# Window attention into a soft mixture of experts: VectorE's small steps in one-tensor form, sink sums scaled once at the end, and new keys for the planner

## The chip, the cores and the metric

The kernel runs on one core of one Trainium2 chip. The metric is the device time of one execution in microseconds; the median of three runs is given with the lowest and the highest. The engines are TensorE (PE in the rows; PEld is its weight load), VectorE (DVE), ScalarE (ACT), GpSimd (POOL), and SyncE (SP), which only issues the transfers.

## The reference, cut to what matters

Everything is float32. Attention has 4 batches, 8 heads, 768 positions and 64 columns a head; a query sees the last 128 positions and the first 4, the sinks. Its output, 3072 tokens of 512 columns, goes through a soft mixture of 8 experts with 4 slots each.

```python
keep = is_sink | in_window                  # n_sink = 4, window = 128
scores = np.where(keep, q @ k.T / 8, -1e9)
a = np.exp(scores - scores.max(-1));  a /= a.sum(-1) + 1e-9
x = (a @ v) as 3072 tokens x 512

logits = x @ phi                            # 3072 x 32 slots
d = softmax(logits, over the tokens)        # 1e-9 added to the sum
slot_input = d.T @ x                        # 32 x 512
slot_out = relu(slot_input[e] @ w1[e]) @ w2[e]      # 512 -> 1024 -> 512, 8 experts
c = softmax(logits, over the slots)         # 1e-9 added to the sum
out = c @ slot_out                          # 3072 x 512
```

## The kernel before, in words

**Jobs.** The 768 positions of a batch are three jobs of 256 tokens, so there are 12 jobs (`window_path`, line 768). A job loads q, k and v, transposes q and k by TensorE (`prep`), and makes four score tiles (`softmax`, line 843), one for each group of four heads (`quad`) and half of the rows (`odd`), each with 68 or 132 window columns next to the sinks'. For a score tile VectorE masks and takes the maximum (`maxima`), ScalarE does four exponentials with their sums (`exps`), VectorE adds EPS to the four sums and takes reciprocals (`inverse`, lines 901 to 903, two tensors of four columns), GpSimd multiplies 128x528 weights by them and copies the sink weights to `sk`. In the first job of a batch VectorE has one or three more steps a tile. Two score tiles of one quad are transposed (`weights_transposed`), copied to `xws`, cut to the window by GpSimd's selections (`select`), and multiplied with v (`values`).

**Tokens.** Each job ends in `tokens` (line 337): logits of 256 tokens, a running minimum of negated maxima `m` (lines 371 to 375), exponentials, a transpose of `lt`, and products with the tokens. `sums` (line 419) keeps `acc[:, 0:256]` as a running weighted sum, scaled by `al` when the maximum moves. The sinks' values are not added to the tokens; their weights are summed in `acc[:, 256:384]` (`far`), 32 columns for each batch, and put in at the end. Before the change all columns of `far` that are in use are scaled by `al` in every job (line 424), so 32 to 128 columns. `totals` keeps the running sum of exponentials `z`. `slot_softmax` (line 519) does the softmax over slots of a finished batch, with an EPS step on six columns (`rs`, line 534). `finish` (line 449) joins the two halves of the partitions, and after it the two expert layers and the output follow (`tail`, line 588), for which 32 weight tiles of 1 MB are loaded, most of them during attention into free slots, the last 14 when attention has given its slots back.

**What sets the order.** Every step of attention is put into a `Plan` with a key, an engine and an estimated time (`add`). `Plan.order` (line 196) is a list scheduler: it goes through the steps by estimated times, takes on each engine the step that can start first, and among those that can start within a small margin the one with the lowest key. The keys are a table (`CFG`, line 706), 4 for each job plus an offset for each kind of step. The result is one fixed order for each engine; on the chip an engine takes its instructions in that order and waits on semaphores. Instructions that are put out this way all have line 156. Two PSUM tiles hold scores (`s`), four hold everything else (`w`), so a step that opens a tile also waits until an older one has been copied out.

Of the kernel before, what the change touches and what calls it, by code (L numbers as in the profile page):

```python
# [8 lines left out]
F32 = mybir.dt.float32  # L9
# [4 lines left out]
AF = mybir.ActivationFunctionType  # L14
ALU = mybir.AluOpType
# [4 lines left out]
P = 128  # L20
# [53 lines left out]
class Sinks:  # L74


    def __init__(self, nc, plan, pool, tmp, c, v, store):

        B = v.shape[0]
        self.nc, self.c, self.store = nc, c, store.rearrange("p (b s) -> p b s", b=B)  # L80
        self.sk = [pool.tile([P, P], F32, name=f"sk{i}") for i in range(2)]
        self.pst = pool.tile([P, P], F32, name="pst")
# [39 lines left out]
        plan.add(1.5, "D", 2.0, load, w=["v4"])  # L122
        plan.add(1.0, "G", 0.6, clear, w=["swide", "vphi", ("sk", 0), ("sk", 1)])
        plan.add(1.0, "G", 0.15, lambda e: nc.gpsimd.tensor_copy(tmp[:, 64:128], v4), r=["v4"], w=["v4b"])
# [183 lines left out]
class Moe:  # L308
# [6 lines left out]
    def __init__(self, nc, c, keep, work, pools, B):  # L315
        self.nc, self.c, self.keep, self.work, self.pools, self.B = nc, c, keep, work, pools, B

        self.lt = keep.tile([P, P], F32, name="lt")
        self.lb = keep.tile([P, 2, 2, 32], F32, name="lb")
        self.spare = keep.tile([P, P], F32, name="spare")  # L320
        self.sel = keep.tile([P, 2, 32], F32, name="sel")
        self.acc = keep.tile([P, 384], F32, name="acc")
        self.sinks = None

        t = keep.tile([P, 7], F32, name="sums")
        self.m, self.z, self.zb, self.al = t[:, 0:2], t[:, 2:3], t[:, 3:5], t[:, 5:7]
        self.n = 0
        self.cs, self.ct = {}, {}
        self.call = keep.tile([P, B, 6, 32], F32, name="call")
        self.si = keep.tile([P, 4, 32], F32, name="si")  # L330

        self.eps = keep.tile([P, 1], F32, name="eps")
        nc.gpsimd.memset(self.eps, 0.0)
        nc.gpsimd.memset(self.eps[64:96], EPS)
        nc.vector.memset(self.z, 0.0)

    def tokens(self, plan, keys, b, j, x, xn, blocks):
# [19 lines left out]
        def logits(e):  # L357
# [12 lines left out]
        key = next(k)  # L370
        plan.add(key, "V", 0.2, lambda e: nc.vector.tensor_reduce(
            new, L["tile"][:, 0:P], op=ALU.max, axis=AX.X, negate=True), r=[L["name"]], w=[("m", n % 2)])
        if n:
            plan.add(key, "V", 0.07, lambda e: nc.vector.tensor_tensor(new, new, old, op=ALU.min),
                     r=[("m", (n + 1) % 2)], w=[("m", n % 2)])
# [10 lines left out]
        else:  # L386
            next(k)
        plan.add(next(k), "P", 0.11, lambda e: nc.tensor.transpose(T["tile"][:, 0:P], lt, c.ident),
                 r=["lt0", "lt1"], w=[T["name"]], new=T)
# [56 lines left out]
        plan.add(next(k), "AV", (0.11, 0.13), logit, r=[T["name"]], w=[("lg", b, j, x) for x in blocks], last=T)  # L446
        plan.add(key, "V", 0.56 if sinks else 0.4, sums, r=[S["name"], aln], w=["acc"], last=S)

    def finish(self, plan, keys):
# [3 lines left out]
        nc, c, work = self.nc, self.c, self.work  # L453
        m, mo = self.m[:, (self.n - 1) % 2:(self.n - 1) % 2 + 1], self.m[:, self.n % 2:self.n % 2 + 1]
        W, Z, SI, D = plan.psum(), plan.psum(), plan.psum(), plan.psum()
        sinks = self.sinks
        f = work.tile([P, 1], F32, name="f")
        rz = self.rz = work.tile([P, 1], F32, name="rz")
# [39 lines left out]
        if sinks:  # L498
            key = next(k)
            plan.add(key, "P", 0.2, far, r=["sf", "acc"], w=["sd"], new=D)  # L500
            plan.add(key, "V", 0.2, lambda e: nc.vector.tensor_tensor(
# [17 lines left out]
    def slot_softmax(self, plan, key, b, names):  # L519
# [17 lines left out]
        plan.add(key, "V", 0.7, sums, w=[n])  # L537
        plan.add(key, "V", 0.3, lambda _: nc.vector.tensor_tensor(
# [143 lines left out]
class Weights:  # L682
# [8 lines left out]
    def load(self, t):  # L691
# [3 lines left out]
        else:  # L695
# [9 lines left out]
PT = 3  # L705
CFG = {'prep': [12.62, 12.36],
       'load': [62.54, -93.04],
       'v': [68.49, 63.17],
       'S': -12.9,
       'M': 126.11,  # L710
       'E': 297.18,
       'N': -191.46,
       'K0': 89.87,
       'T': [-201.07, -298.71],
       'K': -214.45,
       'sel': [89.25, -30.52, -145.68, -195.21],
       'val': [295.22, -19.77, 342.69, 369.69],
       'xn': [-57.94],
       'tok': [357.78, -262.56, 29.9, -50.0, 133.69, -75.28, 36.37, -51.64, -299.8, 208.29, -224.86],
       'sm': -143.04,  # L720
       'sinks': -181.93,
       'tr': [63.06, 25.65, 135.89, 140.0, 109.95, 86.26, 129.98, 2.55, 42.1, 2.21, 118.89, 92.88, 82.47, 53.92,
           125.08, 116.73, 96.95, 0.0, 138.66, 84.47, 128.65, 60.63, 120.33, 77.77, 78.14, 114.47, 21.23],
       'w': [105.83, 8.0],
       'fin': [287.49, -10.46, -125.39, -132.28, 35.33, -56.83, -2.84, 389.2, -90.55, 66.83, 472.81],
       'xn1': [40.22],
       'tok1': [-9.5, -16.36, 75.49, -213.58, -107.33, 247.29, -76.98, 179.88, 150.72, 361.93, -107.59]}


def window_path(ctx, tc, c, moe, q, k, v, phi, w1, w2, out):  # L730
# [31 lines left out]
    pts = [t[:, 528 * i:528 * i + 528].rearrange("p (a y) -> p a y", a=4) for i in range(PT)]  # L762
    small = t[:, 1840:1864].rearrange("p (g x y) -> p g x y", g=3, x=2)
    eps = t[:, 1864:1868]
    qt = fr.tile([P, 4, 256], F32, name="qt")
    nc.vector.memset(eps, EPS)

# [4 lines left out]
    def copy(e, o, i):  # L772
        (nc.scalar.copy if e == "A" else nc.vector.tensor_copy)(o, i)
# [69 lines left out]
    def softmax(keys, n, tl):  # L843
# [5 lines left out]
        s = plan.psum("s")  # L849
        nm, z = small[:, g % 3, 0], small[:, g % 3, 1]  # L850
        pt = pts[g % PT]
# [422 lines left out]
```

## Time and profile before

| | |
|---|---|
| median of 3 runs | 247.46 us (245.77 to 247.46) |
| the profiled execution | 248.19 us |
| its span, from the first to the last instruction | 246.5 us |
| mean granted TensorE clock in the span | 0.965 of full speed |

The four batches run from about 7.5 to 183 us, `finish` with the turning of the slot weights to 194, the expert layers to 232, and the output to 246.5. [...]

### The profile page before, as it was taken

What the parts mean: (1) busy time and instruction counts of PE and PEld (TensorE: products, weight loads), DVE (VectorE), ACT (ScalarE), POOL (GpSimd) and SP (SyncE); (2) the same over time, 40 slices, a digit from 0 to 9 for tenths busy, and PEclk for the clock granted to TensorE, in tenths of its full rate; (3) what the DMA queues carried; (4) which work ended last, traced back from release to release, by engine and by line L of the source; (5) the groups of instructions that cost most, each with busy time, mean ns of one, the idle gap of its engine ahead of it and who ended that gap; (6) DMA issues with size and microseconds to landing.
All of it is one profiled execution on the core that took longest, in us unless ns stands there. A gap on an engine that the chain in (4) does not pass through costs nothing.

```text
span 246.5 us, 9008 instructions
## 1 busy us (share of the span) xinstructions
PE 212.7 (86%) x3547; PEld 151.2 (61%) x3547; DVE 168.9 (69%) x455; ACT 150.4 (61%) x579; POOL 131.7 (53%) x247
## 2 busy tenths in 40 slices
PE   7866998998979799798979998898799999998830
PEld 7754676775657577575757766576578533655520
DVE  3387896789999778999956899999736411324240
ACT  2257699758988866898886579888634212123230
POOL 3048687954777785487776646867894160000000
PEclk9979799999999999999979999999999999999995
DMA  5497997788989778998996998983119999999896
GB/s 124 104 212 168 257 212 206 287 186 244 195 251 282 229 256 174 258 198 236 278 263 195 178 274 194 311 268 134 45 44 350 419 366 357 351 349 370 297 314 214
DMA packets 102965, 59.47 MB, mean 241 GB/s; under 512 B 76292, under 2 KB 98820, under 8 KB 102916
## 3 DMA queue, kind: packets, MB, share of 16 engines
q1 hardware_dynamic: 102916, 58.83, 82.9%
q8 instruction: 30, 0.49, 0.8%
q14 instruction: 19, 0.16, 0.2%
HBM read 52.53 MB, written 6.29 MB: 239 GB/s over the span
## 4 chain that ended last, share of the span: by engine, by line
PE 50%; DVE 21%; ACT 14%; DMA 5%; issue 4%; POOL 2%; ACTq 0%; DVEq 0%; POOLq 0%
PE w L156 35%; PE s L156 14%; ACT wt L156 11%; DVE wt L156 8%; DVE s L156 7%; DMA wt<-in_moe_w_dram 5%; DVE sums L156 2%; DVE first L156 2%; PE w L1226 2%; POOL wt L156 1%; DVE acc L156 1%; DVE rs L156 1%; ACT first L156 1%; ACT wt L659 0%; ACT lt L156 0%
## 5 line engine op out<-in xcount | busy, mean ns | idle before, releaser
L156 ACT ACTIVATE wt<-s,wt 128x132 f32<-128x132 f32 x192 | 68.9, 382 | 11.0 <-PE s L156 4.6
L156 POOL TENSOR_TENSOR wt<-wt 128x528 f32<-128x528 f32 x48 | 51.2, 1066 | 28.3 <-DVE wt L156 10.0
L156 POOL TENSOR_SCALAR_AFFINE_SELECT wt<-wt 128x512 f32<-128x512 f32 x88 | 54.0, 639 | 18.8 <-ACT wt L156 12.8
L156 PE MATMUL w<-wt 128*64 128x128 f32 (+2 forms) x548 | 51.3, 324 | 4.3 <-DVE wt L156 2.6
L156 PE MATMUL s<-wt,qt 64*64 64x196 f32 (+2 forms) x768 | 44.4, 332 | 6.7 <-ACT wt L156 5.5
L156 PEld LDWEIGHTS w<-wt 128*64 128x64 f32 (+1 forms) x548 | 37.0, 144 | 16.2 <-POOL wt L156 4.4
L156 ACT ACTIVATION_READ_ACCUMULATOR wt<-s,wt 128x1 f32 x192 | 41.6, 217 | 0.0
L156 ACT COPY wt<-w 128x512 f32<-128x512 f32 (+1 forms) x50 | 28.0, 573 | 12.8 <-PE w L156 9.2
L156 DVE TENSOR_REDUCE wt<-s 128x4 f32<-128x528 f32 x48 | 33.9, 707 | 1.7
L156 PEld LDWEIGHTS s<-wt,qt 64*64 64x64 f32 x768 | 26.0, 135 | 14.3 <-ACT wt L156 7.9
L156 PE MATMUL w<-ident,first 64*128 64x64 f32 x576 | 27.1, 229 | 0.6 <-ACT qt L156 0.2
L156 PEld LDWEIGHTS w<-ident,first 64*128 64x128 f32 x576 | 21.5, 139 | 9.6 <-issue 4.8
L156 PE MATMUL w<-ident,wt 64*128 64x64 f32 (+1 forms) x419 | 24.2, 237 | 3.1 <-POOL wt L156 2.0
L156 PEld LDWEIGHTS w<-ident,wt 64*128 64x128 f32 (+1 forms) x419 | 18.7, 144 | 10.8 <-issue 5.6
L156 DVE COPY first<-w 128x512 f32<-128x512 f32 x28 | 18.8, 678 | 7.2 <-PE w L156 7.2
L156 DVE COPY_PREDICATED s<-later,s 128x256 f32<-128x256 uint8 x48 | 20.2, 421 | 2.1 <-PE s L156 1.1
L156 DVE COPY wt<-w 128x512 f32<-128x512 f32 (+3 forms) x27 | 16.8, 623 | 6.8 <-ACT wt L156 4.3
L156 ACT ACTIVATE qt<-w 128x512 f32<-128x512 f32 (+1 forms) x23 | 13.2, 581 | 9.3 <-PE s L156 7.9
L156 PE MATMUL s<-wt 128*32 128x256 f32 x240 | 15.4, 381 | 0.9 <-DMA wt<-in_moe_w_dram 0.9
L156 ACT COPY first<-w 128x512 f32<-128x512 f32 x20 | 11.6, 605 | 7.0 <-PE w L156 7.0
L156 DVE TENSOR_TENSOR wt<-wt 128x4 f32<-128x4 f32 x48 | 13.6, 284 | 2.2 <-POOL wt L156 1.0
L156 PE MATMUL w<-wt,si 128*32 128x512 f32 x120 | 14.1, 594 | 0.2 <-DVE si L156 0.2
(130 smaller groups left out, 255.9 us busy)
## 6 DMA issues: line engine op xcount, KB each, us to landing
wt<-in_moe_w_dram SPq DMA_DIRECT2D x30, 1024.0 KB, 8.0
wt<-in_v_dram SPq DMA_DIRECT2D x24, 256.0 KB, 4.8
first<-in_q_dram SPq DMA_DIRECT2D x22, 256.0 KB, 3.9
first<-in_k_dram SPq DMA_DIRECT2D x22, 256.0 KB, 4.7
out_dram<-wt SPq DMA_DIRECT2D x4, 1024.0 KB, 8.6
first<-in_moe_w_dram SPq DMA_DIRECT2D x2, 1024.0 KB
out_dram<-wt SPq DMA_DIRECT2D x3, 512.0 KB
first<-in_k_dram SPq DMA_DIRECT2D x4, 128.0 KB, 2.4
```

What stands on the lines that cost most here:

```text
L156: return self.tc.keep_in_program_order(f(*args, **kw))
L1226: nc.tensor.matmul(t[:, 0:P], lhsT=c.ident, rhs=c.ident, start=True, stop=True)
```

## The change: what it does

Five things in the small steps, and a new table.

- EPS is added by `tensor_scalar`, with the constant in the instruction, where it was a `tensor_tensor` with a tensor of constants. It covers six columns, the four sums and two more, read as 3x2 and written as 2x3; the same form is used for the six columns in `slot_softmax`.
- The running minimum `min(new, old)` and the totals `z * al + zb` become `tensor_scalar` steps with the second operand as a per-partition scalar. `m` gets a column for each job, and keeps them all.
- `far` is no longer scaled in every job. Inside a batch the 32 columns of that batch are scaled in the step that adds to them. At the end the exponential `f` is taken for the last maximum of each of the four batches, and GpSimd multiplies `far`, 128x128, by it; the product with `sel` then follows. The column of `m` after the last batch's takes the place that `old` had.
- `sk` has 64 columns instead of 128, so 64 rows are transposed and copied to `pst`, and the lower half of `pst` is cleared once.
- Estimated times of seven steps are changed, and all keys in `CFG` but `w`.

```diff
-        self.sk = [pool.tile([P, P], F32, name=f"sk{i}") for i in range(2)]
+        self.sk = [pool.tile([P, 64], F32, name=f"sk{i}") for i in range(2)]
...
-            for t in self.sk:
-                nc.gpsimd.memset(t, 0.0)
+            nc.gpsimd.memset(self.pst[64:128], 0.0)
...
-        old, new = self.m[:, (n + 1) % 2:(n + 1) % 2 + 1], self.m[:, n % 2:n % 2 + 1]
+        old, new = self.m[:, n - 1:n], self.m[:, n:n + 1]
...
-            plan.add(key, "V", 0.07, lambda e: nc.vector.tensor_tensor(new, new, old, op=ALU.min),
+            plan.add(key, "V", 0.07, lambda e: nc.vector.tensor_scalar(new, new, old, None, op0=ALU.min),
...
-                if n:
-                    z1 = 32 * (b + (j > 0))
-                    nc.vector.tensor_scalar(far[:, 0:z1], far[:, 0:z1], al, None, op0=ALU.mult)
                 if j:
-                    nc.vector.tensor_tensor(d, d, S["tile"][:, 256:288], op=ALU.add)
+                    nc.vector.scalar_tensor_tensor(d, d, al, S["tile"][:, 256:288], op0=ALU.mult, op1=ALU.add)
...
-                nc.vector.scalar_tensor_tensor(z[64:128], z[64:128], al[64:128], zb[64:128],
-                                               op0=ALU.mult, op1=ALU.add)
+                nc.vector.tensor_scalar(z[64:128], z[64:128], al[64:128], zb[64:128], op0=ALU.mult, op1=ALU.add)
...
-        plan.add(next(k), "A", 0.3, lambda e: nc.scalar.activation(f, m, AF.Exp, bias=mo, scale=-1.0), r=mm, w=["f"])
+        plan.add(next(k), "A", 0.3, lambda e: nc.scalar.activation(
+            fb, self.m[:, each - 1:self.n:each], AF.Exp, bias=mo, scale=-1.0), r=mm, w=["f"])
...
-            nc.tensor.matmul(D["tile"][:, 0:64], lhsT=self.acc[:, 256:384], rhs=s2, start=True, stop=True)
+            nc.tensor.matmul(D["tile"][:, 0:64], lhsT=swap, rhs=sel.rearrange("p h s -> p (h s)"), start=True, stop=True)
...
+            plan.add(key, "G", 0.3, lambda e: nc.gpsimd.tensor_tensor(
+                self.si, self.acc[:, 256:384].rearrange("p (b s) -> p b s", b=self.B),
+                fb.unsqueeze(2).to_broadcast([P, self.B, 32]), op=ALU.mult), r=["f", "acc"], w=["far"])
...
-            nc.vector.tensor_scalar(rs, rs, EPS, None, op0=ALU.add)
+            nc.vector.tensor_scalar(rs.rearrange("p (x y) -> p x y", x=2), rs.rearrange("p (x y) -> p x y", x=3),
+                                    EPS, None, op0=ALU.add)
...
-            nc.vector.tensor_tensor(z, z, eps, op=ALU.add)
+            nc.vector.tensor_scalar(z6.rearrange("p (x y) -> p x y", x=2), z6.rearrange("p (x y) -> p x y", x=3),
+                                    EPS, None, op0=ALU.add)
...
-       'S': -12.9,
+       'S': -115.04,
```

The order in TensorE's queue, in the middle job of the third batch (some 121 to 130 us in the profile). `s<-wt,qt` is a score tile, `w<-ident,first_76` the transposes of q or k, `w<-ident,wt` the transposes of attention weights, `w<-wt` the values, `w<-ident,sk_165` and `w<-ident,lt` the transposes of sink weights and of `lt`, `w<-first_77,lb` the products with the tokens. Before:

```order
L156 MATMUL s<-wt,qt 64x196 x8
L156 MATMUL w<-ident,first_76 128x64 x16
L156 MATMUL s<-wt,qt 64x196 x8
L156 MATMUL w<-ident,wt 128x64 x16
L156 MATMUL w<-ident,sk_165 128x128
L156 MATMUL w<-ident,lt 128x128
L156 MATMUL w<-wt 64x2x2x64 x2
L156 MATMUL w<-wt 64x2x64 x4
```

The same place now, from the same score tile on:

```order
L155 MATMUL s<-wt,qt 64x196 x8
L155 MATMUL w<-wt 64x2x2x64 x2
L155 MATMUL w<-wt 64x2x64 x4
L155 MATMUL w<-wt 64x2x2x64 x2
L155 MATMUL w<-wt 64x2x64 x4
L155 MATMUL w<-ident,wt 128x64 x16
L155 MATMUL w<-ident,sk_165 64x128
L155 MATMUL w<-ident,lt 128x128
L155 MATMUL s<-wt,qt 64x196 x8
L155 MATMUL w<-ident,first_76 128x64 x16
L155 MATMUL w<-first_77,lb 32x256
```

The values of the first four heads (the four rows of `w<-wt`) have moved ahead, from behind the transpose of `lt` to right behind a score tile, ahead of the second transposes of attention weights; a score tile and the transposes of q and k that stood ahead of `lt` now stand behind it.

VectorE's queue at the end of a batch, where the softmax over slots of the batch before is done. `acc` holds the running sums, `wt<-wt` the EPS step and the reciprocals, `rs` the six sums of the slot softmax. Before:

```order
L156 TENSOR_SCALAR acc<-acc,sums 128x64
L156 TENSOR_TENSOR acc<-acc,w 128x32
L156 SCALAR_TENSOR_TENSOR acc<-acc,sums,w 128x256
L156 TENSOR_TENSOR wt<-wt 128x4
L156 RECIPROCAL wt<-wt 128x4
L156 TENSOR_REDUCE rs<-call 128x6
L156 TENSOR_SCALAR rs<-rs 128x6
L156 RECIPROCAL rs<-rs 128x6
```

Now:

```order
L155 SCALAR_TENSOR_TENSOR acc<-acc,sums,w 128x32
L155 SCALAR_TENSOR_TENSOR acc<-acc,sums,w 128x256
L155 TENSOR_SCALAR wt<-wt 128x6
L155 RECIPROCAL wt<-wt 128x4
L155 TENSOR_SCALAR qt<-w 128x2x4x64
L155 TENSOR_SCALAR wt<-wt 128x6
L155 RECIPROCAL wt<-wt 128x4
L155 TENSOR_REDUCE rs<-call 128x6
L155 TENSOR_SCALAR rs<-rs 128x6
L155 RECIPROCAL rs<-rs 128x6
```

The scaling of `acc` is gone and the addition behind it carries the scalar; the EPS steps are `TENSOR_SCALAR` on six columns; a scaling of q (`qt<-w`) and another EPS step now stand ahead of the slot softmax.

## Rows read from the trace of the kernel before

**Rows 1.** The page, part 1: busy time of each engine, its share of the span, and instructions.
```profile
PE 212.7 (86%) x3547; PEld 151.2 (61%) x3547; DVE 168.9 (69%) x455; ACT 150.4 (61%) x579; POOL 131.7 (53%) x247
```
**Rows 2.** Busy time by stretch, one stretch for each of the four batches, cut where a batch's first score tile starts (us from the span's start): length, busy us of PE, of its weight loads (PEld), of DVE, ACT and POOL with their instructions, the granted TensorE clock as a share of full speed, the DMA engines' busy share, GB/s.
```profile
7.50:50.22 42.72, 37.21 (x705) 27.75 (x706) 33.20 (x89) 29.25 (x122) 28.59 (x51) 0.92 0.83 207
50.22:93.11 42.89, 38.37 (x740) 28.38 (x741) 37.35 (x98) 34.55 (x138) 29.62 (x53) 1.00 0.86 235
93.11:137.34 44.23, 39.98 (x738) 29.42 (x740) 37.27 (x98) 34.61 (x138) 29.56 (x52) 0.96 0.89 230
137.34:182.87 45.53, 40.59 (x753) 29.76 (x751) 39.47 (x102) 35.08 (x144) 32.41 (x58) 1.00 0.65 180
```
**Rows 3.** The same view for the third batch, cut in two.
```profile
93.11:126.13 33.02, 28.86 (x549) 20.93 (x549) 30.73 (x79) 27.66 (x111) 21.05 (x37) 1.00 0.91 227
126.13:137.34 11.21, 11.11 (x189) 8.48 (x191) 6.54 (x19) 6.95 (x29) 8.51 (x16) 0.85 0.83 238
```
**Rows 4.** The chain of work that ended last, in order of time: start us, us, engine, tile written, line. The pieces on small VectorE steps, and the last long wait.
```profile
73.96 0.98 DVE rs L156
...
79.39 1.05 DVE sums L156
...
116.58 0.98 DVE rs L156
...
122.02 1.04 DVE sums L156
...
157.50 0.60 DVE wt L156
...
158.88 0.74 DVE acc L156
...
171.11 0.60 DVE wt L156
171.91 0.91 DVE acc L156 x3
...
216.09 11.39 DMA wt<-in_moe_w_dram
```
**Rows 5.** Groups of VectorE instructions: line, engine, operation, out<-in by tile names, out<-in as partitions x elements (of the first shape, where a group has several), count | busy us, mean ns of one | idle before.
```profile
L156 DVE TENSOR_TENSOR wt<-wt 128x4 f32<-128x4 f32 x48 | 13.6, 284 | 2.2 <-POOL wt L156 1.0 <-ACT wt L156 0.9
L156 DVE TENSOR_TENSOR sums<-sums 128x1 f32<-128x1 f32 x11 | 7.2, 659 | 0.4
L156 DVE SCALAR_TENSOR_TENSOR acc<-acc,sums,w 128x256 f32<-128x256 f32 x11 | 5.2, 474 | 0.2 <-issue 0.2
L156 DVE TENSOR_SCALAR acc<-acc,sums 128x32 f32<-128x32 f32 (+3 forms) x11 | 5.2, 469 | 0.0
L156 DVE TENSOR_SCALAR rs<-rs 128x6 f32<-128x6 f32 x4 | 3.1, 770 | 0.1
L156 DVE SCALAR_TENSOR_TENSOR sums<-sums 64x1 f32<-64x1 f32 x11 | 2.4, 219 | 1.2 <-ACT lt L156 0.9
L156 DVE TENSOR_TENSOR acc<-acc,w 128x32 f32<-128x32 f32 x8 | 1.5, 188 | 1.3 <-PE w L156 0.6
```
**Rows 6.** Timeline, VectorE (DVE) and GpSimd (POOL) side by side at three places: start us, us, engine, line, operation, tiles and shapes, count [idle before <- what ended it].
```profile
116.45 1.07 POOL L156 TENSOR_TENSOR wt<-wt 128x528 f32<-128x528 f32 x1 [0.48 <-DVE wt L156]
116.58 0.97 DVE L156 TENSOR_SCALAR rs<-rs 128x6 f32<-128x6 f32 x1
...
190.31 0.46 POOL L156 TENSOR_TENSOR qt<-call,qt 128x128 fp32r<-128x128 f32 x1
190.31 0.27 DVE L156 TENSOR_SCALAR rz<-sums,f,eps 128x1 f32<-128x1 f32 x1
190.50 0.31 DVE L156 TENSOR_SCALAR lt<-sel,f 128x64 f32<-128x64 f32 x1
...
195.61 0.17 DVE L156 TENSOR_SCALAR rs<-rs 128x6 f32<-128x6 f32 x1
```
**Rows 7.** Who TensorE (PE) waited for: us in total, times, longest us.
```profile
PE s L156 <- ACT wt L156: 5.5, 8, 1.0
PE w L156 <- DVE pst L156: 3.0, 3, 1.2
...
PE w L156 <- ACT lt L156: 2.3, 3, 1.5
```
**Rows 8.** Timeline of PE at two places in the third and fourth batch.
```profile
124.62 0.30 PE L156 MATMUL w<-ident,sk 128*128 128x128 f32 x1
126.13 0.33 PE L156 MATMUL w<-ident,lt 128*128 128x128 f32 x1 [1.21 <-DVE pst L156]
126.39 3.48 PE L156 MATMUL w<-wt 128*64 128x256 f32 x24
...
171.04 0.89 PE L156 MATMUL s<-wt,qt 64*64 64x196 f32 x16 [0.38 <-ACT wt L156]
172.33 1.96 PE L156 MATMUL w<-wt 128*64 128x256 f32 x24 [0.39 <-POOL wt L156]
```
**Rows 9.** Busy time by stretch around the end of attention, columns as in Rows 2.
```profile
168.00:184.00 16.00, 13.68 (x241) 10.06 (x241) 10.86 (x30) 10.20 (x41) 13.91 (x27) 1.00 0.12 31
188.00:216.00 28.00, 27.43 (x295) 14.53 (x298) 8.81 (x32) 5.91 (x20) 6.02 (x13) 1.00 1.04 372
```
**Rows 10.** Timeline of the DMA queue on SyncE: start us, us that the issues took, tiles, count.
```profile
182.87 2.80 SPq L156 DMA_DIRECT2D wt<-in_moe_w_dram  x4
```

More of the change, by code (lines that the diff above doesn't have):

```diff
@@ L122, in __init__ @@
         plan.add(1.5, "D", 2.0, load, w=["v4"])
-        plan.add(1.0, "G", 0.6, clear, w=["swide", "vphi", ("sk", 0), ("sk", 1)])
+        plan.add(1.0, "G", 0.6, clear, w=["swide", "vphi", "pst"])
         plan.add(1.0, "G", 0.15, lambda e: nc.gpsimd.tensor_copy(tmp[:, 64:128], v4), r=["v4"], w=["v4b"])
@@ L323, in __init__ @@
         self.sinks = None
-        t = keep.tile([P, 7], F32, name="sums")
-        self.m, self.z, self.zb, self.al = t[:, 0:2], t[:, 2:3], t[:, 3:5], t[:, 5:7]
+        t = keep.tile([P, 5 + 3 * B + 1], F32, name="sums")
+        self.z, self.zb, self.al, self.m = t[:, 0:1], t[:, 1:3], t[:, 3:5], t[:, 5:6 + 3 * B]
         self.n = 0
@@ L370, in tokens @@
         key = next(k)
-        plan.add(key, "V", 0.2, lambda e: nc.vector.tensor_reduce(
+        plan.add(key, "V", 0.24, lambda e: nc.vector.tensor_reduce(
             new, L["tile"][:, 0:P], op=ALU.max, axis=AX.X, negate=True), r=[L["name"]], w=[("m", n % 2)])
         if n:
-            plan.add(key, "V", 0.07, lambda e: nc.vector.tensor_tensor(new, new, old, op=ALU.min),
+            plan.add(key, "V", 0.07, lambda e: nc.vector.tensor_scalar(new, new, old, None, op0=ALU.min),
                      r=[("m", (n + 1) % 2)], w=[("m", n % 2)])
@@ L387, in tokens @@
             next(k)
-        plan.add(next(k), "P", 0.11, lambda e: nc.tensor.transpose(T["tile"][:, 0:P], lt, c.ident),
+        plan.add(next(k), "P", 0.16, lambda e: nc.tensor.transpose(T["tile"][:, 0:P], lt, c.ident),
                  r=["lt0", "lt1"], w=[T["name"]], new=T)
@@ L446, in tokens @@
         plan.add(next(k), "AV", (0.11, 0.13), logit, r=[T["name"]], w=[("lg", b, j, x) for x in blocks], last=T)
-        plan.add(key, "V", 0.56 if sinks else 0.4, sums, r=[S["name"], aln], w=["acc"], last=S)
+        plan.add(key, "V", 0.55 if sinks else 0.4, sums, r=[S["name"], aln], w=["acc"], last=S)
     def finish(self, plan, keys):
@@ L453, in finish @@
         nc, c, work = self.nc, self.c, self.work
-        m, mo = self.m[:, (self.n - 1) % 2:(self.n - 1) % 2 + 1], self.m[:, self.n % 2:self.n % 2 + 1]
+        m, mo = self.m[:, self.n - 1:self.n], self.m[:, self.n:self.n + 1]
+        each = self.n // self.B
         W, Z, SI, D = plan.psum(), plan.psum(), plan.psum(), plan.psum()
         sinks = self.sinks
-        f = work.tile([P, 1], F32, name="f")
+        fb = work.tile([P, self.B], F32, name="f")
+        f = fb[:, self.B - 1:self.B]
         rz = self.rz = work.tile([P, 1], F32, name="rz")
@@ L499, in finish @@
             key = next(k)
-            plan.add(key, "P", 0.2, far, r=["sf", "acc"], w=["sd"], new=D)
+            plan.add(key, "G", 0.3, lambda e: nc.gpsimd.tensor_tensor(
+                self.si, self.acc[:, 256:384].rearrange("p (b s) -> p b s", b=self.B),
+                fb.unsqueeze(2).to_broadcast([P, self.B, 32]), op=ALU.mult), r=["f", "acc"], w=["far"])
+            plan.add(key, "P", 0.2, far, r=["fsel", "far"], w=["sd"], new=D)
             plan.add(key, "V", 0.2, lambda e: nc.vector.tensor_tensor(
@@ L533, in sums @@
             nc.vector.reduce_sum(rs, e, axis=AX.X)
-            nc.vector.tensor_scalar(rs, rs, EPS, None, op0=ALU.add)
+            nc.vector.tensor_scalar(rs.rearrange("p (x y) -> p x y", x=2), rs.rearrange("p (x y) -> p x y", x=3),
+                                    EPS, None, op0=ALU.add)
             nc.vector.reciprocal(rs, rs)
-        plan.add(key, "V", 0.7, sums, w=[n])
+        plan.add(key, "V", 0.8, sums, w=[n])
         plan.add(key, "V", 0.3, lambda _: nc.vector.tensor_tensor(
@@ L705 @@
 PT = 3
-CFG = {'prep': [12.62, 12.36],
-       'load': [62.54, -93.04],
-       'v': [68.49, 63.17],
-       'S': -12.9,
[L710 to L723, printed above, removed]
+CFG = {'prep': [-3.73, -7.0],
+       'load': [0.46, -428.98],
+       'v': [7.74, 3.29],
+       'S': -115.04,
+       'M': 718.72,
+       'E': 1322.67,
+       'N': -75.85,
+       'K0': 31.16,
+       'T': [-339.17, -595.64],
+       'K': -285.3,
+       'sel': [-5.04, -200.0, -383.99, -1007.74],
+       'val': [-107.55, -214.89, 322.25, 132.7],
+       'xn': [-332.17],
+       'tok': [144.73, -116.92, -979.6, -778.5, -344.49, -105.13, -350.16, 137.16, -1629.96, -74.14, 490.19],
+       'sm': -932.4,
+       'sinks': -391.46,
+       'tr': [124.03, 52.03, 127.84, 57.95, 67.55, 99.05, 140.0, 101.82, 89.63, 4.44, 12.53, 8.73, 53.92, 110.96,
+           65.83, 4.35, 23.97, 119.7, 126.05, 16.24, 113.23, 49.39, 84.86, 67.65, 0.0, 24.53, 115.51],
        'w': [105.83, 8.0],
-       'fin': [287.49, -10.46, -125.39, -132.28, 35.33, -56.83, -2.84, 389.2, -90.55, 66.83, 472.81],
-       'xn1': [40.22],
-       'tok1': [-9.5, -16.36, 75.49, -213.58, -107.33, 247.29, -76.98, 179.88, 150.72, 361.93, -107.59]}
+       'fin': [-580.79, -346.71, 51.07, -445.39, -122.03, -358.66, -188.2, 444.45, 209.77, 673.01, 355.17],
+       'xn1': [-365.55],
+       'tok1': [-918.42, -491.6, 242.3, -332.63, -294.4, 729.29, -894.49, 361.24, 84.18, -10.6, -793.66]}
 def window_path(ctx, tc, c, moe, q, k, v, phi, w1, w2, out):
@@ L762, in window_path @@
     pts = [t[:, 528 * i:528 * i + 528].rearrange("p (a y) -> p a y", a=4) for i in range(PT)]
-    small = t[:, 1840:1864].rearrange("p (g x y) -> p g x y", g=3, x=2)
-    eps = t[:, 1864:1868]
+    small = t[:, 1840:1870].rearrange("p (g y) -> p g y", g=3)
     qt = fr.tile([P, 4, 256], F32, name="qt")
-    nc.vector.memset(eps, EPS)
+    nc.vector.memset(t[:, 1840:1870], 1.0)
     jobs = [(b, j) for b in range(B) for j in range(NJ)]
@@ L849, in softmax @@
         s = plan.psum("s")
-        nm, z = small[:, g % 3, 0], small[:, g % 3, 1]
+        nm, z, z6 = small[:, g % 3, 0:4], small[:, g % 3, 4:8], small[:, g % 3, 4:10]
         pt = pts[g % PT]
@@ L890, in maxima @@
                                     negate=True)
-        add(keys["M"], "V", 1.1 + (0.55 * (1 - odd) + 0.15) * (j == 0), maxima, r=[sn], w=[sn, nn])
+        add(keys["M"], "V", 1.08 + (1.1 - 0.8 * odd) * (j == 0), maxima, r=[sn], w=[sn, nn])
         def exps(e):
@@ L928, in sinks_transposed @@
         h = plan.psum()
-        add(key, "P", 0.15, lambda e: nc.tensor.transpose(h["tile"][:, 0:P], sinks.sk[n % 2], c.ident),
-            r=[("sk", n % 2)], w=[h["name"]], new=h)
-        add(key, "AV", (0.17, 0.2), lambda e: copy(e, sinks.pst, h["tile"][:, 0:P]), r=[h["name"]], w=["pst"], last=h)
+        add(key, "P", 0.15, lambda e: nc.tensor.transpose(h["tile"][0:64, 0:P], sinks.sk[n % 2], c.ident),
+            r=[("sk", n % 2)], w=[h["name"]], new=h, mode=HALVES)
+        add(key, "AV", (0.17, 0.2), lambda e: copy(e, sinks.pst[0:64], h["tile"][0:64, 0:P]),
+            r=[h["name"]], w=["pst"], last=h)
     def select(key, n, quad, i):
```

## The prediction

> **What bounds the kernel now.** I read the page's busy shares first, then busy time by stretch, then the chain of waits, then the groups of small VectorE steps, and last a timeline with VectorE and GpSimd side by side. No engine is full over the span: PE has 86%, VectorE 69%, GpSimd 53% [rows 1]. Cut by batch it looks different. Each of the four batches takes 43 to 46 us, and PE is busy in 37.2 to 40.6 of them; the idle rest is 5.5, 4.5, 4.3 and 4.9 us, 19.2 together [rows 2]. Inside the third batch the idle time lies in one place: from 93.1 to 126.1 us VectorE is busy for 30.7 of 33.0 us and PE for 28.9, and behind that PE is busy for 11.1 of 11.2 [rows 3]. So for three quarters of a batch VectorE sets the pace, and then PE does.
>
> The reader is to see next what VectorE does with that time. Adding a constant to four numbers takes 284 ns on average, taking the smaller of two columns 659, adding a constant to six columns 770, scaling a few columns of the far sums 469 [rows 5]. The same step on six columns took 0.17 us at 195.6 us, where GpSimd had nothing to do, and 0.97 at 116.6, where it began 0.13 us into a GpSimd multiplication of 1.07 and ended with it (116.45 + 1.07 = 117.52, against 117.55) [rows 6]. These are waits for GpSimd, not work. Several stand in the chain that ended last: 0.98 twice, 1.05 and 1.04, 0.60 twice, 0.74 and 0.91 [rows 4].
>
> Behind attention the end hangs on the weights. The chain's last long piece is a wait of 11.4 us for a weight transfer [rows 4]; the DMA engines are busy at 0.12 of their time from 168 to 184 us, since every slot is taken, and at full share from 188 to 216 [rows 9]. So attention's end releases the transfers (the last fourteen weight tiles begin at 182.9 us [rows 10]), and what attention saves is saved at the end, as long as the earlier transfers are done by then; the 16 nearly idle us before 184 are room for that.
>
> **The change, part by part.** The sum is made against the profiled execution, 248.19 us; the median shown is 0.73 lower.
>
> *Small steps in a plain form.* 48 additions of EPS now read six columns as 3x2 and write them as 2x3; I price one at 0.17, the undisturbed step on six columns [rows 6]. Bounds: 0.17, since undisturbed it is the same work, and 0.28, today's mean, if they still wait. 48 x (0.284 - 0.173) = 5.3 us of VectorE. The 11 minima become a one-column step whose second operand is a per-partition scalar. The nearest rows are 219 ns for the one-column step with one such scalar [rows 5] and 0.27 with two, at 190.31, which ran while a GpSimd multiplication ran beside it from 190.31 to 190.77 and did not wait [rows 6]; I take 0.22, bounds 0.17 (the quickest small step on SBUF columns in these rows) and 0.66. 11 x (0.659 - 0.22) = 4.8. The four steps on six columns in the slot softmax go from 0.77 to 0.17: 2.4. The running totals get two scalars instead of one: 0.27 for 0.22, 11 x 0.05 = 0.6 more.
>
> [...] The row at 190.31 shows such a step not waiting [rows 6]. [...]
>
> *Far sums.* 11 scalings of 0.469 go, 5.2 us; eight additions at 0.19 take a scalar along, between 0.19 and the 0.47 of the same form on 256 columns [rows 5], taken at 0.22, near the one with 32 columns: 0.2 more. In their place GpSimd multiplies 128x128 once at the end, like the 0.46 at 190.31 [rows 6], with a hop on either side some 0.5 us on the way to the first layer. I cost it at nothing: the weights' transfer is the late one there [rows 4, 9]; without that cover it costs 0.5.
>
> VectorE so sheds 5.3 + 4.8 + 2.4 - 0.6 + 5.2 - 0.2 = 16.9 of 168.9 us. What counts is what stood on the path. From the chain [rows 4]: two steps on rs, 2 x (0.98 - 0.17) = 1.6; two minima, 1.05 + 1.04 - 2 x 0.22 = 1.65; two EPS steps, 2 x (0.60 - 0.17) = 0.85; two scalings of acc, 0.74 and about 0.45 of the 0.91, 1.2; less some five totals at 0.05, 0.25. Together 5.0. PE is next: in the stretch of 33.0 us it has only 4.2 to give.
>
> *The order.* All keys are new. In the middle of a batch a column of score tiles stood close together, and the transpose of lt came straight behind two prep and score steps; now a value step stands between, and score tiles are spread. Three waits can be read off. The transpose of lt waits 1.21 us for the copy of pst, queued on VectorE; this kind is 3.0 in three times, of the 2.3 for lt about 0.7 lie in the steps that moved [rows 7, 8]: 3.7 can go. Score tiles wait 5.5 for ScalarE [rows 7]; I take a third, 1.8, since ScalarE's own work stays. Against it, the values of the first four heads now stand only four steps behind their weights' transposes, in eight jobs. Before, one job has that order, and there PE waited 0.39 us for GpSimd [rows 8]: 8 x 0.39 = 3.1 paid. Net -2.4; bounds +3 (nothing won, all paid) and -8 (all 3.7 and 5.5 won, little paid).
>
> *The rest.* Two clears of sk become one half clear on GpSimd at the start, and transposes and copies of sink rows cover 64 instead of 128 rows: same columns, nothing. [...]
>
> Sum: -5.0 - 2.4 = -7.4, so 240.8 in its own execution and 240.1 against the median of 247.46.
>
> **The rivals.** *PE fills up.* If VectorE's 16.9 us and the even order let two thirds of the 19.2 idle us go, 12.8 leave: 234.7. For it: PE was 99% busy wherever VectorE wasn't in the way [rows 3]. Against: PE is one queue in order, and its steps wait on chains through three engines.
>
> [...]
>
> *Absorbed.* The shed time lies beside PE's work and the order brings nothing: 2 us or less, 245.5 to 247.5. For it: 12 of the 16.9 us are not in the chain.
>
> *GpSimd late, slower.* Behind the transposes stand two copies and up to four selections, and now only a score step, transposes, logits and a score step cover them. If one multiplication of 1.07 us [rows 6] stands ahead of them in GpSimd's queue, each of the eight waits is 0.39 + 1.07 = 1.46, 11.7 in all; less 5.0 and 3.7, with nothing won for ScalarE the end comes 3.0 later: 250.5. It decides from a mean wait of 1.1 us (8.7 / 8). Against: GpSimd has 13 free us in each batch [rows 2].
>
> **How the numbers follow.** Within 1%, 245.0 to 249.9, is what a measurement of this kernel can hardly tell from no change. Chances: the forecast with its own range of 237 to 243, 0.50; PE fills up, 0.15; steps that still wait, 0.13; absorbed, 0.13; slower, 0.09. The first three are faster by over 1% but for a little of the third: 0.77 faster, 0.14 within, 0.09 slower. The range runs from 234.5, the filled PE, to 246.5, which takes in the steps that still wait and half of the absorbed.
>
> **What would show it.** Right: VectorE's busy time near 152 us; no EPS step, minimum or rs step above 0.3 us; batches of 40 to 41.5 us; the last weight tiles requested near 175.5 us instead of 182.9; the part behind that as long as it was. Wrong: a mean of the EPS steps near 0.28; PE's waits for GpSimd in front of values over 8 us; a batch still over 42; or a released tail that is longer by what attention saved, for then the transfers were the bound.

## The result, and the profile after

The changed kernel takes 234.68 us (median of 4 runs, 233.64 to 235.58) against 246.62 beside it: 0.9523 of the time, interval 0.9449 to 0.9597. Two later comparisons gave 0.9498 and 0.9423. That is some 12 us less, where 7.4 were forecast. Ratios here and below leave out disturbed executions (two of those further down took 329.63 and 384.3 us), so a ratio can differ a little from the quotient of two medians, which take in all executions. The profiled execution took 235.58 us, of which the span is 233.9.

First the page's busy shares of the changed kernel, which answer to [rows 1].

```profile
PE 207.8 (89%) x3545; PEld 148.9 (64%) x3545; DVE 150.2 (64%) x437; ACT 151.0 (65%) x586; POOL 133.0 (57%) x247
```

VectorE lost 18.7 us of busy time, PE 4.9. Then the four batches, columns as in [rows 2], and behind them the DMA queue's row for the first two of the last weight tiles, which answers to [rows 10].

```profile
7.00:46.67 39.67, 34.60 (x635) 25.89 (x635) 30.43 (x82) 26.68 (x112) 24.65 (x45) 0.91 0.80 192
46.67:87.34 40.67, 37.95 (x740) 28.23 (x741) 31.52 (x92) 34.70 (x139) 29.84 (x52) 1.00 0.91 248
87.34:124.78 37.44, 37.02 (x739) 27.84 (x742) 31.59 (x91) 34.62 (x140) 29.83 (x52) 1.00 1.02 260
124.78:170.68 45.90, 42.56 (x823) 31.71 (x823) 35.25 (x102) 37.97 (x155) 36.77 (x64) 1.00 0.79 216
```

```profile
170.68 1.55 SPq L155 DMA_DIRECT2D wt<-in_moe_w_dram  x2
```

What matters most is the third batch: PE is busy for 37.02 of 37.44 us, while VectorE has 5.9 us free. Beside [rows 2] the batches are 3.1, 2.2 and 6.8 us shorter and the fourth 0.4 longer (it now holds 823 matrix products for 753, since the new order puts its first score tile further ahead). PE's idle time in the four fell from 19.2 to 11.6 us (5.1, 2.7, 0.4 and 3.3). The weights are requested at 170.68 instead of 182.87, and from there to the end it is 63.2 us (before 63.6): what attention saved was saved at the end.

Next the small steps of VectorE, columns as in [rows 5].

```profile
L155 DVE TENSOR_SCALAR wt<-wt 128x6 f32<-128x6 f32 x48 | 9.3, 195 | 0.2
L155 DVE TENSOR_SCALAR sums<-sums 128x1 f32<-128x1 f32 x11 | 2.3, 206 | 0.3
L155 DVE TENSOR_SCALAR sums<-sums 64x1 f32<-64x1 f32 x11 | 3.0, 276 | 1.4 <-ACT lt L155 1.0
L155 DVE TENSOR_SCALAR rs<-rs 128x6 f32<-128x6 f32 x4 | 1.1, 271 | 0.1
L155 DVE SCALAR_TENSOR_TENSOR acc<-acc,sums,w 128x32 f32<-128x32 f32 x8 | 1.9, 238 | 0.4 <-PE w L155 0.4
```

The means are near those forecast. But three places in the timeline (VectorE and GpSimd side by side, as in [rows 6]) show that this isn't because the EPS form no longer waits.

```profile
71.79 0.16 DVE L155 TENSOR_SCALAR wt<-wt 128x6 f32<-128x6 f32 x1
72.30 1.07 POOL L155 TENSOR_TENSOR wt<-wt 128x528 f32<-128x528 f32 x1 [0.80 <-DVE wt L155]
73.03 0.37 DVE L155 TENSOR_SCALAR rs<-rs 128x6 f32<-128x6 f32 x1
...
110.07 1.07 POOL L155 TENSOR_TENSOR wt<-wt 128x528 f32<-128x528 f32 x1
110.42 0.74 DVE L155 TENSOR_SCALAR wt<-wt 128x6 f32<-128x6 f32 x1
```

At 73.03 the step on rs begins inside GpSimd's multiplication and ends 0.03 us behind it (73.40 against 73.37); at 110.42 an EPS step does the same (111.16 against 111.14). The one at 71.79 takes 0.16 because GpSimd stands idle: the multiplication that comes next is the one that waits for this step. Of the 48, only 5 take more than 0.2 us.

Last, who PE waited for, which answers to [rows 7], and behind it, from the timeline, GpSimd's selections and the values of the first four heads in one job: the place at which the forecast paid.

```profile
PE s L155 <- ACT wt L155: 2.8, 5, 1.0
PE w L155 <- ACT lt L155: 1.5, 1, 1.5
PE w L155 <- POOL wt L155: 1.5, 1, 1.5
PE w L155 <- DVE pst L155: 0.7, 1, 0.7
```

```profile
113.11 2.52 POOL L155 TENSOR_SCALAR_AFFINE_SELECT wt<-wt 128x512 f32<-128x512 f32 x4
115.68 1.96 PE L155 MATMUL w<-wt 128*64 128x256 f32 x24
```

The one wait of 1.5 us for GpSimd's wt is in front of a transpose at the very start (12.94), not at values. The selections end at 115.63 and the values start at 115.68, just in time, without a wait.

### The profile page after: what moved, and what is told of

The parts are those of the page before. It is cut to its first block, busy times and chain, and to the rows that moved or that the text cites. A ratio compares the mean times of both kernels' runs of the same rounds, so it can differ in the third digit from the quotient of the medians.

```text
span 233.9 us, 8934 instructions
## 1 busy us (share of the span) xinstructions
PE 207.8 (89%) x3545; PEld 148.9 (64%) x3545; DVE 150.2 (64%) x437; ACT 151.0 (65%) x586; POOL 133.0 (57%) x247
## 4 chain that ended last, share of the span: by engine, by line
PE 69%; DVE 9%; DMA 8%; ACT 5%; issue 3%; POOL 2%; SPq 0%; DVEq 0%; POOLq 0%; ACTq 0%
PE w L155 49%; PE s L155 18%; DMA wt<-in_moe_w_dram 5%; ACT wt L155 3%; DVE s L155 3%; DVE wt L155 3%; DMA wt<-in_v_dram 2%; PE w L1229 2%; POOL wt L155 1%; DVE sums L155 1%; DVE first L155 1%; ACT wt L661 1%; ACT qt L155 0%; ACT pst L155 0%; DVE phi L155 0%
## 5 line engine op out<-in xcount | busy, mean ns | idle before, releaser
L155 POOL TENSOR_TENSOR wt<-wt 128x528 f32<-128x528 f32 x48 | 51.2, 1066 | 27.1 <-DVE wt L155 10.5
L155 PE MATMUL w<-wt 128*64 128x128 f32 (+2 forms) x548 | 49.6, 316 | 2.8 <-DVE wt L646 1.2
L155 PE MATMUL s<-wt,qt 64*64 64x196 f32 (+2 forms) x768 | 45.9, 337 | 5.2 <-ACT wt L155 2.8
L155 PEld LDWEIGHTS w<-wt 128*64 128x64 f32 (+1 forms) x548 | 35.4, 140 | 15.8 <-POOL wt L155 2.5
L155 ACT ACTIVATION_READ_ACCUMULATOR wt<-s,wt 128x1 f32 x192 | 41.5, 216 | 0.0
L155 ACT COPY wt<-w 128x512 f32<-128x512 f32 (+1 forms) x48 | 27.4, 578 | 13.6 <-PE w L155 10.2
L155 PEld LDWEIGHTS s<-wt,qt 64*64 64x64 f32 x768 | 26.9, 137 | 12.8 <-ACT wt L155 3.9
L155 DVE COPY wt<-w 128x512 f32<-128x512 f32 (+3 forms) x29 | 18.2, 627 | 16.0 <-PE w L155 11.8
L155 ACT COPY first<-w 128x512 f32<-128x512 f32 x33 | 19.0, 598 | 10.4 <-PE w L155 10.1
L155 PE MATMUL w<-first,phi 128*32 128x128 f32 x384 | 13.0, 276 | 0.0
L155 ACT ACTIVATE qt<-w 128x512 f32<-128x512 f32 (+1 forms) x19 | 11.0, 585 | 2.5 <-PE s L155 1.6
L155 PEld LDWEIGHTS s<-wt 128*32 128x32 f32 x240 | 7.9, 110 | 7.1 <-DMA wt<-in_moe_w_dram 1.3
```

Of the source, the lines that this page charges most:

```text
L155: return self.tc.keep_in_program_order(f(*args, **kw))
```

## The experiments

The question was where the extra 4 to 5 us came from: from the small steps (the forecast gave them 5.0) or from the order (2.4). The code is shortened throughout.

**Steps and order apart.** Two kernels, each with one half of the change. In the first, the keys and time estimates of before are put back; in the second, the steps of before run under the new keys and estimates. The estimated times that differ between the two kernels are five, not seven. But for the clears at the start and the finish, whose far sums differ, the queues of PE and GpSimd stand in the traces as in the kernel whose order is used. So does ScalarE's with the order alone. With the steps alone three of its copies of transposed weights stand with VectorE instead (26 copies of 128x512 to `wt` for 23 before, 2.0 us): the planner may give such a copy to either engine.

```
steps_old_order: the changed kernel, with
-CFG = {'prep': [-3.73, -7.0], ...
+CFG = {'prep': [12.62, 12.36], ...          (and the five estimates of before)
order_old_steps: the kernel before, with
-CFG = {'prep': [12.62, 12.36], ...
+CFG = {'prep': [-3.73, -7.0], ...           (and the five new estimates and the mode of the sink transposes)
```

Of the steps alone was expected: 

> All new small steps (EPS in 3x2 to 2x3, minima with a scalar operand, far sums scaled once by GpSimd, half-height sink rows), but the keys and time estimates of the kernel before, so that the queues of PE, ScalarE, GpSimd and SP stand as they did before. If the two parts of the forecast simply add, the steps are worth 5.0 us: 241.6 against 246.6. If the steps carry nearly all (VectorE was the pace and PE fills up in any order): 235 to 237. If the order carries nearly all: 244 to 246.

Of the order alone: 

> All old small steps, but the keys and time estimates of the changed kernel, so that the queues of PE, ScalarE, GpSimd and SP stand as they do after. If the two parts add, the order is worth 2.4 us: 244.2. If the order carries nearly all: 236 to 239. If the order rests on the quick steps (values placed close behind their weights' transposes then wait for GpSimd, whose multiplications wait for the slow EPS steps): 245 to 250, with PE's waits for GpSimd above the 7.5 us of before.

Of the changed kernel beside them: 

> The changed kernel once more, beside its own variants: 233.6 to 235.6 under every theory.

Measured against 247.12 us: the steps alone 243.25, 0.9885 (0.9849 to 0.9921); the order alone 236.67, 0.9641 (0.9566 to 0.9715); both 233.62, 0.9498 (0.9435 to 0.9561). So by the ratios the steps are worth 2.8 us, the order 8.9 and both 12.4: they add nearly, with the sizes the other way round. The split is rough, since it hangs on the kernel before: by the medians alone the steps come to 3.9 and the order to 10.5. Without the kernel before, the order is worth 9.6 us with the new steps (243.25 to 233.62), and the steps 3.1 in the new order (236.67 to 233.62). That the order rests on the quick steps is out. VectorE's groups show what either half does, first the steps alone, then the order alone; `first<-w` are the copies of transposed q and k.

```profile
L155 DVE TENSOR_SCALAR wt<-wt 128x6 f32<-128x6 f32 x48 | 15.7, 328 | 3.6 <-ACT wt L155 2.4 <-POOL wt L155 1.0
L155 DVE TENSOR_SCALAR sums<-sums 128x1 f32<-128x1 f32 x11 | 2.4, 214 | 0.4
L155 DVE TENSOR_SCALAR rs<-rs 128x6 f32<-128x6 f32 x4 | 0.8, 195 | 0.1
L155 DVE COPY first<-w 128x512 f32<-128x512 f32 x28 | 18.8, 676 | 4.2 <-PE w L155 4.2
```

```profile
L156 DVE TENSOR_TENSOR wt<-wt 128x4 f32<-128x4 f32 x48 | 9.7, 201 | 0.2
L156 DVE TENSOR_TENSOR sums<-sums 128x1 f32<-128x1 f32 x11 | 2.5, 231 | 0.3
L156 DVE TENSOR_SCALAR acc<-acc,sums 128x32 f32<-128x32 f32 (+3 forms) x11 | 3.6, 325 | 0.0
L156 DVE TENSOR_SCALAR rs<-rs 128x6 f32<-128x6 f32 x4 | 1.1, 270 | 0.1
L156 DVE SCALAR_TENSOR_TENSOR sums<-sums 64x1 f32<-64x1 f32 x11 | 4.8, 437 | 1.5 <-ACT lt L156 1.1
L156 DVE COPY first<-w 128x512 f32<-128x512 f32 x15 | 10.1, 676 | 3.3 <-PE w L156 3.2
```

In the old order the new EPS form takes 328 ns, more than the old form's 284 [rows 5]. In the new order most old forms have little wait left: 284 to 201, 659 to 231, 770 to 270. The totals go the other way: 219 before, 437 in the new order, where they meet GpSimd's steps (the one at 116.13 takes 1.04 us and ends at 117.17, a multiplication at 117.16). Counted in the timelines, 18 of the 48 EPS steps took more than 0.2 us before, 26 with the steps alone, 7 with the order alone and 5 with both. The order, not the form, took most of the waits away. The order does one more thing: 13 of the 28 copies of transposed q and k that VectorE made before, 8.7 us, are now ScalarE's, while four more scalings of q, 2.7 us, have come to VectorE. The minimum is a step whose form did take the wait away. Its place in the old order, with the new form, is the twin of the 1.05 us at 79.39 in [rows 4]; timeline of the steps alone:

```profile
77.21 1.07 POOL L155 TENSOR_TENSOR wt<-wt 128x528 f32<-128x528 f32 x1 [0.41 <-DVE sums L155]
77.24 0.21 DVE L155 TENSOR_SCALAR sums<-sums 128x1 f32<-128x1 f32 x1
```

It begins 0.03 us into the multiplication and is done in 0.21 us.

**Does the EPS step's shape matter, and do its waits carry the order's gain?** In the built changed kernel the contiguous 3x2 and 2x3 stand merged: its trace records a run of six read and a run of six written, though the views print 128x6 for either shape. With the unmerged strides below it records three pairs read and two triples written. Three kernels in the order of before: without the step, with strides that can't be merged, and with five columns in one run.

```
-nc.vector.tensor_scalar(z6 as 2x3, z6 as 3x2, EPS, None, op0=ALU.add)
no_eps_old_order: (nothing)
+odd_old_order:  nc.vector.tensor_scalar(zo[2 rows of 4][:, :, 0:3], zi[3 rows of 3][:, :, 0:2], EPS, ...)
+five_old_order: nc.vector.tensor_scalar(z5, z5, EPS, None, op0=ALU.add)
```

Without it: 

> The new small steps in the order of before, without the 48 EPS additions (each sum holds a term exp(0) = 1, and 1 + 1e-9 is 1 in fp32). In the old order these steps took 15.7 us of VectorE (48 x 0.328). If the order's gain of about 8.9 us comes through VectorE (in the new order its small steps find GpSimd idle, so they don't wait), taking the waiting steps out of the old order must bring most of it: 235 to 238. If the gain is PE's own sequence (fewer waits for the copies of pst, for ScalarE, for the weights), the old order stays at 241 to 243.

Unmerged: 

> The new small steps in the order of before, the EPS addition with strides that can't be merged: three pairs at distance 3 read, two triples at distance 4 written. In the built changed kernel the contiguous 3x2 and 2x3 stand as one run of six. If the shape on the engine decides whether the step waits for GpSimd: mean 0.16 to 0.18 us instead of 0.328, and the time within 1 us of the kernel without the steps plus at most 48 x 0.17 of VectorE. If every such step waits, whatever its shape: 0.30 to 0.33, and 241 to 244.

Five: 

> The new small steps in the order of before, the EPS addition over five columns in one run (odd, and the same for source and destination) instead of six. If an odd count alone frees the step from waiting: mean 0.16 to 0.18 us and a time as with the unmerged strides. If odd but equal waits as even does: 0.30 to 0.33 us and 241 to 244.

Measured against 247.47 us: without 237.64, 0.9619 (0.9588 to 0.9650); unmerged 240.03, 0.9708 (0.9671 to 0.9745); five 243.33, 0.9841 (0.9812 to 0.9870). The groups, unmerged and then five:

```profile
L155 DVE TENSOR_SCALAR wt<-wt 128x6 f32<-128x6 f32 x48 | 7.3, 152 | 3.2 <-ACT wt L155 3.2
```

```profile
L155 DVE TENSOR_SCALAR wt<-wt 128x5 f32<-128x5 f32 x48 | 16.0, 333 | 3.6 <-ACT wt L155 2.4 <-POOL wt L155 1.0
```

The same step at the same place, in the timeline of the steps alone and then of the unmerged form:

```profile
106.21 0.64 POOL L155 TENSOR_SCALAR_AFFINE_SELECT wt<-wt 128x512 f32<-128x512 f32 x1
106.33 0.54 DVE L155 TENSOR_SCALAR wt<-wt 128x6 f32<-128x6 f32 x1
```

```profile
106.04 0.63 POOL L155 TENSOR_SCALAR_AFFINE_SELECT wt<-wt 128x512 f32<-128x512 f32 x1
106.13 0.15 DVE L155 TENSOR_SCALAR wt<-wt 128x6 f32<-128x6 f32 x1
```

As one run of six it ends with GpSimd's selection (106.87 against 106.85); unmerged it is done in 0.15 us in the middle of one. So at this place the shape that reaches the engine decides (0.54 us against 0.15; over the 48 steps a mean of 328 ns against 152), and the change's own shape never reached it. The run of five, which waits as the run of six does, gained 3.9 us; the unmerged form, which doesn't wait, some 7 (0.9708). So in the old order the waits of the EPS steps are worth 3.3 us (243.33 to 240.03), and the steps themselves, without a wait, another 2.4 (240.03 to 237.64). Without the step the old order comes to 0.9619, as good as the new order with all the old steps (0.9641). The windows of its two middle batches, beside those of the steps alone:

```profile
48.74:88.56 39.82, 37.65 (x738) 27.87 (x735) 32.32 (x84) 33.54 (x137) 29.68 (x51) 1.00 0.95 254
88.56:128.38 39.82, 37.65 (x739) 27.87 (x735) 32.33 (x84) 33.53 (x137) 29.67 (x51) 1.00 0.96 246
```

```profile
49.04:90.11 41.07, 38.10 (x737) 28.14 (x734) 35.49 (x96) 33.53 (x137) 29.77 (x52) 1.00 0.89 245
90.11:131.17 41.06, 38.11 (x738) 28.14 (x734) 35.48 (x96) 33.53 (x137) 29.68 (x52) 1.00 0.97 245
```

Each batch is 1.25 us shorter, with 3.2 us less of VectorE. It is still 2.2 us longer than PE is busy.

**The small steps in the new order.** Five kernels with the changed kernel's order, each with one thing undone or taken further.

```
eps_two:        +nc.vector.tensor_tensor(z, z, eps, op=ALU.add)
far_each:       +nc.vector.tensor_scalar(far[:, 0:z1], far[:, 0:z1], al, None, op0=ALU.mult)   (in each step; plain additions)
min_totals_two: +nc.vector.tensor_tensor(new, new, old, op=ALU.min)   (and the totals with one scalar)
odd:            the unmerged EPS step as above
no_eps:         without the EPS step
```

> The changed kernel with its order, only the 48 EPS additions as a step of two SBUF tensors again (four columns plus four columns). If VectorE's time is now cover (64% busy, PE the bound): within 1 us of the changed kernel, 234 to 236. If the EPS steps stand on the path to GpSimd's multiplication and so to PE's transposes of the weights: 48 x 0.1 to 0.12 us come back in part, 237 to 240, and PE's waits for GpSimd rise from 4.1 to 8 us or more. Their mean should go from 195 ns to 280 or more under both.

> The changed kernel with its order, but the far sums scaled in each step again (11 scalings) and added plainly; GpSimd's multiplication at the end uses one factor. If the far sums carry the difference of about 3 us between old and new small steps in the new order: 235.5 to 237. If VectorE's time is cover there: within 1 us of the changed kernel, 233 to 235, with scalings of 0.26 to 0.5 us, 3 to 5 us of VectorE in all.

> The changed kernel with its order, but the 11 minima as a step of two tensors and the 11 totals with one scalar and one tensor, as before. In the new order with all old steps these took 231 and 437 ns against 206 and 276 now: 11 x 0.19 = 2 us of VectorE. If they are what the new small steps are worth in the new order (3 us between old and new steps there): 235 to 236.5. If nothing of it is on the path: 233 to 235.

> The changed kernel with its order and the EPS additions in strides that can't be merged (pairs read, triples written). In the new order these steps took 195 ns, 40 more than the 152 that the unmerged form took: 2 us of VectorE, nearly all beside PE's work: 232.5 to 235. A time under 232 would say that the few long steps (up to 0.74 us) stand on the path.

> The changed kernel with its order, without the 48 EPS additions (each sum holds exp(0) = 1, so 1e-9 is lost in fp32). Beside the old order without them (0.962 of before) it shows what the order is worth where these steps can't wait. If the order works only by keeping small steps off GpSimd's: no better than the old order without them by over 1 us, 236 to 238. If PE's own sequence is worth something as well: 232 to 234. VectorE loses 9.3 us of busy time; if that time is cover, as the run with the two-tensor form suggests, the time is that of the changed kernel within 1 us.

The changed kernel beside the last three: 

> The changed kernel a third time, beside these variants: 233 to 235.5 under every theory, 0.945 to 0.955 of before.

Measured: two-tensor EPS 234.16, 0.9525 (0.9445 to 0.9606); far sums in each step 234.42, 0.9473 (0.9438 to 0.9508); old minima and totals 233.02, 0.9428 (0.9371 to 0.9485); unmerged EPS 234.53, 0.9483 (0.9425 to 0.9542); no EPS 232.86, 0.9443 (0.9394 to 0.9492); the changed kernel a third time 232.48, 0.9423 (0.9387 to 0.9459). All lie within what three comparisons of the changed kernel itself spread over (0.9423 to 0.9523), the first 0.0002 above it. In the new order no single step can be told from nothing, the unmerged form included, which came out 2.0 us above the changed kernel beside it with intervals that overlap. Yet all new steps together were worth 3.1 us there (236.67 to 233.62), with 4.8 us less of VectorE; which of them carry it, no run shows. The changed kernel itself came out a little under the 0.945 expected of it. For the two-tensor EPS step the row says why:

```profile
L155 DVE TENSOR_TENSOR wt<-wt 128x4 f32<-128x4 f32 x48 | 9.3, 195 | 0.2
```

It takes no longer than the new form, where 280 ns or more were expected under either theory, and PE's weight loads waited 4.1 us for GpSimd in both. The expectation overlooked that the order keeps these steps off GpSimd's, whatever their form. The old minimum took 151 ns there, where 231 were expected and the new form takes 206: without a wait the old form is the quicker one. No version can be told from the changed kernel as quicker.

The kernel without EPS steps, beside its twin in the old order, also says what the order is worth where these waits can't exist: 0.9443 against 0.9619, 4.3 us (some 3 to 6 by the two intervals). Its middle batches:

```profile
47.10:85.41 38.31, 37.20 (x739) 27.83 (x735) 30.11 (x80) 34.65 (x140) 30.03 (x52) 1.00 0.96 263
85.41:122.77 37.36, 36.95 (x739) 27.83 (x735) 29.79 (x79) 34.68 (x141) 29.86 (x52) 1.00 1.02 262
```

Here PE's idle time is 1.1 and 0.4 us for 2.2 in the old order. The unmerged form, which doesn't wait either, gives a second such pair: 0.9708 and 0.9483, 5.6 us. So some 4 to 6 us of what the order brings, about half, have nothing to do with waits of the EPS steps. That this half is PE's own sequence is not shown: VectorE is busy for 30.1 and 29.8 us in these batches and for 32.3 in the old order, since 8 of its 14 copies of transposed q and k in the two batches have gone to ScalarE and 3 scalings of q have come for them. No run has the new sequence of PE with the old sharing of the copies. The halves are rough: each ratio has 0.3 to 0.6 per cent to either side.

## Why the prediction was right, and where its sizes were wrong

*The range.* It held narrowly: the 234.68 us lie 0.2 above its lower end, two later medians of the changed kernel (233.62 and 232.48) below it. The forecast's own range, 237 to 243, was missed; the wider one held because it took in the filled PE, to which the prediction gave a chance of 0.15. That is partly luck.

*What bounds the kernel.* Right: with VectorE out of the way PE filled up, 37.02 of 37.44 us in the third batch, as the 11.1 of 11.2 in [rows 3] had said.

*EPS steps at 0.17.* This step of the working failed. It took the six columns at 195.6 us, where GpSimd had nothing to do [rows 6], for the price of a form. The row at 116.58 in the same group, one tensor and six columns too, had waited (0.97 us); that was the evidence that counted. In the old order the steps went from 13.6 to 15.7 us, so the 0.85 us booked on the path wasn't there. That the mean in the new order, 0.195, came out near 0.17 is the order's doing and luck for this term. Of the chance of 0.13 for steps that still wait no run shows the time that it stands for; what the runs showed in its place is waits in the runs of six, EPS (0.74 us at 110.42) and rs (0.37 at 73.03), those of EPS worth 3.3 us in the old order, and none in the minima (0.21 at 77.24).

*Minima, totals, rs.* Minima 0.206 for 0.22 and totals 0.276 for 0.27: right, and the one-column step does not wait (0.21 us at 77.24), as the row at 190.31 had shown. The steps on rs: 0.27 for 0.17, since two of the four met a multiplication (0.37 us each; the other two took 0.17).

*Far sums.* Their 5 us of VectorE went as worked out, and the multiplication at the end is hidden (63.2 us behind the request, 63.6 before). In the new order nothing of it can be measured: 0.9473 with the scalings put back.

*Direct part, 5.0 us.* Measured some 3 to 4: 2.8 (2.0 to 3.7) for the new steps in the old order, 3.9 (3.2 to 4.7) with the run of five, whose steps wait as long. With the 0.85 of the EPS steps taken out the working gives 4.2. That these steps became 2.1 us longer, and that VectorE had three copies more there, 2.0 us, leaves room for the rest; how much of it was on the path was not measured.

*Order, 2.4 us net.* The term that was mis-sized: 8.9 (7.0 to 10.7) alone. The 3.1 us paid at the values never came: the eight-fold 0.39 was one row of one job [rows 8], and in the new order the selections are done just before (115.63 against 115.68). The waits booked as won came to 3.7 us for 5.5 booked, less than half of the 8.9; who PE waited for with the order alone, beside [rows 7]:

```profile
PE s L156 <- ACT wt L156: 3.0, 6, 1.0
PE w L156 <- ACT lt L156: 2.8, 1, 2.8
PE w L156 <- DVE pst L156: 1.3, 2, 0.7
```

Two things were missing. New keys also decide which small step meets a step of GpSimd: with the order alone VectorE is busy for 155.0 us (168.9 before, 162.1 with the steps alone), and the small steps are 9.8 of the 13.9 that it lost, the totals' added waits counted. And new keys decide which engine makes a copy, which accounts for about the other 4. In the old order the waits of the EPS steps alone were worth 3.3 us; how the rest of the order's gain divides between the copies, the other waits and PE's own sequence stays open.

*PE fills up.* This rival gave 234.7, by two thirds of 19.2 idle us. The time came out there, and its mechanism with it, though not by its sum: of the 11.7 us that the four batches are shorter, 7.6 are idle time (19.2 to 11.6) and 4.0 are PE's busy time. Some of the latter is clock: with the wait of 1.21 us in it the third batch had a granted clock of 0.96 [rows 2, 3], where it is now 1.00, and 24 value products take 1.96 us at a granted clock of 1.00 for 3.48 at 0.54, 1.5 less. The other 2.5 are open. In middle batches at a granted clock of 1.00 PE's busy time for some 738 products was 38.4 before [rows 2], 38.1 with the steps alone, 37.7 without EPS in the old order, and 38.0 and 37.0 in the second and third batch now; its idle time beside them was 4.5, 3.0, 2.2, 2.7 and 0.4, so it falls with the waits. No run shows why.

*What was to show it.* VectorE near 152 us (150.2), the tail as long as it was, PE's waits for GpSimd under 8 us: as said. No step above 0.3 us: not so (0.74, 0.37). Batches of 40 to 41.5 us: 39.7, 40.7, 37.4 and 45.9, of which the last is over the 42 that were to speak against the forecast; it holds 70 products more than before. The weights at 175.5: they came at 170.68, and the sum fell short by about what lies between.

## What to carry to other kernels

When a small step takes several times its usual length, find the step of the other engine with which it ends (here 0.97 us for 0.17, with a multiplication of GpSimd [rows 6]), and ask two things apart: whether another shape, as it stands in the built program, runs beside that step (here a mean of 152 ns for 328), and whether the order can keep the two from meeting (here 201 ns for 284, with the old form). A new order changes which steps meet, on engines that it wasn't made for too, so its worth isn't read from the waits of the bounding engine alone. A planner that may choose the engine also moves work between engines, so count each engine's copies before and after. And once the bounding engine is nearly full (here 37.02 of 37.44 us), a single saving elsewhere (here 7 us of VectorE without the EPS steps) can be worth nothing that can be measured, though several together still showed 3.1 us.

## What the runs showed of the hardware

In the old order a VectorE step with one SBUF tensor and a constant waited for GpSimd's running step as one run of six columns (328 ns mean) and of five (333), and did not with three pairs read and two triples written in strides that can't be merged (152). What it is in GpSimd's step that they wait for, no run shows. The minima, one column with a column as second operand, didn't wait in the new form (0.21 us at 77.24, inside a multiplication of 1.07). Reciprocals ran beside GpSimd without waiting as well: with the unmerged form in the old order 27 of the 48 began inside a selection or multiplication of GpSimd, and none took more than 0.18 us.
